# A Fourier filter and an expert layer on one core: the first batch on one filter tensor, its deferred loads, and new places in the plan

## The chip, the cores and the metric

The kernel runs on one core of a Trainium2 chip. The metric is the device time of one execution in microseconds (us), as the median of several runs. A profile records one execution: its span is shorter than the time by about 2 us. The engines of a core are PE (TensorE, matmuls), DVE (VectorE), ACT (ScalarE), POOL (GpSimd) and SP, which here only issues DMAs; PEld is TensorE's loading of weights, which overlaps PE. The granted clock is the share of TensorE's full clock that it was given.

## The reference, cut to what matters

```python
# x: 8 x 3008 x 256; filt_r, filt_i: 1505 x 256; w_in: 256 x 2048; w_out: 2048 x 256
X = np.fft.rfft(x, axis=1)
y = np.fft.irfft(X * (filt_r + 1j * filt_i), n=3008, axis=1)
h = y.reshape(24064, 256) @ w_in
g = h * (1.0 / (1.0 + np.exp(-beta * h)))
out = g @ w_out                                  # 24064 x 256, float32
```

## The kernel before

Both transforms are matmuls with sine tables, in two factors (3008 = 47 x 64). The expert layer is a main loop of 752 steps: 47 blocks of 512 tokens times 16 slices of the hidden width. A step is two matmuls into `hps`, a Silu on ACT giving `gT`, and, two steps later, four matmuls into `acc`. After 16 steps DVE copies `acc` to `ost` and it is stored. These stores serve below as milestones: store n is the start of DVE's first copy for block n.

The transforms of batches 1 to 7 are cut into units and placed between the steps by a plan: `s1` (first factor), a trip through DRAM (`d1`, read back as `a2`), `s23` (second factor, filter, inverse of it), a trip through `d2` (read as `zz`), `s4`. The views leave buffer numbers out: `a<-d` is the read of `a2` from `d1`, `zz<-d` that of `zz` from `d2`. Batch 0 has nothing to hide behind; it is computed first, with transposes in place of the DRAM trips.

```python
VLAG = 2                                  # s23: the inverse comes two units after the product
# start-up, in program order on POOL: loads of x, then these, then keep
for g in range(NG):
    load_filters(g, 0, nc.sync)           # both filter tensors, lower partitions
    load_filters(g, M, nc.gpsimd)         # both again, upper partitions (6.3 MB in all)
...                                       # w_in, four more issues on POOL
gp.tensor_scalar(keep[:], m_p[:], -1.0, float(M - 1), ALU.mult, ALU.add)
gp.tensor_tensor(keep[:], keep[:], m_p[:], ALU.mult)
gp.tensor_scalar(keep[:], keep[:], 0.5, None, ALU.is_gt)
...
def product(i):                           # batch 0: one product with each filter tensor
    ...
    nc.vector.tensor_tensor(p_t[:], pss[0][:], fr_sb[:, 2 * i : 2 * i + 2, :], ALU.mult)
    ...                                   # i == 0: q_t with keep
    nc.vector.tensor_tensor(q_t[:], pss[1][:], fi_sb[:, 2 * i : 2 * i + 2, :], ALU.mult)
...                                       # inverse3: p_t and q_t both times the one table t3
scale_wout(ws[0], 0, WG, nc.gpsimd); ...  # POOL; after the second of four, load_x(1)
...
place(1, 13, uz(1), per=1)                # rest of batch 0
place(14, 30, uz(2), per=1)
place(31, 50, uz(3), per=2)
place(16, 30, u1(1), per=2)               # batch 1
place(37, 37, [lambda: a2_read(1)], per=9)
place(41, 63, u23(1), True, per=2)
place(68, 68, [lambda: zz_read(1)], per=9)
place(71, 78, u4(1), per=2)
place(50, 70, u1(2), per=3)               # batch 2; x(b+1) is loaded at the end of u1(b)
```

## Time and profile before

| | before |
|---|---|
| time, median | 837.5 us (836.96 to 840.61, 3 runs) |
| span of the profiled run | 839.9 us |
| first `hps` matmul | 51.6 us |
| stores 7 to 43 (36 blocks) | 576.8 us |

Three lines of the page of the kernel before: the span; busy time and share of an engine; and the clock granted to PE in 40 slices of the span, in tenths of full speed.

```profile
span 839.9 us, 15300 instructions
PE 784.3 (93%) x5975; PEld 552.2 (66%) x6071; DVE 410.9 (49%) x670; ACT 585.7 (70%) x885; POOL 185.6 (22%) x200
...
PEclk9879999799999999999999999999999999999999
```

PE is the bound, but the clock dips early. Busy time by stretches of the kernel before shows where PE is idle (start:end in us, then the length; busy us of PE, PEld, DVE, ACT and POOL with counts; granted clock, DMA share, GB/s).

```profile
20.00:30.00 10.00, 2.96 (x27) 2.40 (x26) 1.63 (x5) 2.35 (x4) 5.46 (x11) 0.67 1.06 267
...
50.00:55.00 5.00, 4.61 (x28) 2.66 (x26) 1.98 (x4) 2.34 (x4) 5.00 (x9) 0.50 0.68 198
...
51.56:171.29 119.73, 99.15 (x714) 66.01 (x728) 69.47 (x110) 62.78 (x95) 51.47 (x49) 0.91 0.58 140
...
205.00:302.30 97.30, 95.18 (x726) 67.28 (x737) 51.90 (x81) 71.84 (x109) 19.39 (x20) 1.00 0.41 114
```

The third line runs from the first `hps` to the fifth store: PE is idle for 119.73 - 99.15 = 20.6 us there. The fourth is one steady batch: only 2.1 us idle.

In time order (start, duration, engine, line, operation; in brackets the idle time before it and what ended it), first POOL, then DVE of the kernel before:

```profile
27.05 0.71 POOL L203 DMA_DIRECT2D win_sb<-in_moe_w_in_dram  x1 [0.90 <-DMA fi_sb<-in_filt_i_dram]
27.85 0.18 POOL L230 TENSOR_SCALAR keep<-m_p 128x1 f32<-128x1 f32 x1
...
28.39 0.23 POOL L232 TENSOR_SCALAR keep<-keep 128x1 f32<-128x1 f32 x1
```

```profile
19.59 0.69 DVE L401 TENSOR_TENSOR pb_t<-ps,fr_sb 128x512 bf16<-128x512 f32 x1 [1.50 <-DMA fr_sb<-in_filt_r_dram]
...
28.66 0.48 DVE L403 SCALAR_TENSOR_TENSOR qb_t<-ps2q,keep,fi_sb 128x256 bf16<-128x256 f32 x1 [8.37 <-POOL keep L232]
...
45.67 0.68 DVE L408 TENSOR_TENSOR qb_t<-ps2q,fi_sb 128x512 bf16<-128x512 f32 x1
```

A 0.2 us operation holds DVE for 8.4 us, because POOL first issues twenty DMAs, and many of these wait for earlier ones to land. The chain of waits of the kernel before, followed back from the end, goes through the filters and not through `keep`:

```profile
15.55 17.22 DMA fi_sb<-in_filt_i_dram
...
32.79 10.36 DMA fi_sb<-in_filt_i_dram
```

Last, who PE waited for, as total, number and longest wait: from 52 to 205 us (two lines), then from 205 us to the end (the only line).

```profile
PE ps L489 <- DMA zz<-d: 10.1, 1, 10.1
...
PE ps L556 <- DMA a<-d: 2.4, 1, 2.4
```

```profile
PE ps L584 <- POOL v_t L574: 7.7, 6, 1.3
```

### The profile page before, as it was taken

The page shows a single profiled execution, that of the slowest core. Times are in us where ns is not written, and L with a number is a line of the kernel's source. Part 1 is how long each engine was busy: PE and PEld are TensorE (multiplying, and loading weights), DVE is VectorE, ACT ScalarE, POOL GpSimd, SP SyncE. Part 2 cuts the span into 40 slices and gives each one's busy share as a digit, 9 for nine tenths or more (in the row PEclk, how much of TensorE's full clock was granted, in tenths as well). Part 3 has the DMA queues.
Part 4 walks back from the last instruction along what each step waited for, and adds up shares of the span by engine and source line. Part 5 has one row for each costly group of instructions (what it writes and reads, how often), then busy time and mean ns, then how long its engine had stood idle before and what let it go on. Part 6 is the DMA issues. An engine that isn't in the chain of part 4 may idle for free.

```text
span 839.9 us, 15300 instructions
## 1 busy us (share of the span) xinstructions
PE 784.3 (93%) x5975; PEld 552.2 (66%) x6071; DVE 410.9 (49%) x670; ACT 585.7 (70%) x885; POOL 185.6 (22%) x200
## 2 busy tenths in 40 slices
PE   7589879599999999999999999999999999999997
PEld 4556645376667766777667866677667766766664
DVE  7536488367453656436562664536464463410101
ACT  6546556277767876678767777678766787677775
POOL 6279243023200431013210231003200232000000
PEclk9879999799999999999999999999999999999999
DMA  9962815912391118701293115911183022410101
GB/s 194 251 154 65 212 64 114 218 60 102 98 254 69 46 63 180 215 27 64 88 232 119 67 67 120 249 52 64 45 197 124 26 89 81 84 51 26 51 27 50
DMA packets 87426, 91.44 MB, mean 109 GB/s; under 512 B 4585, under 2 KB 76282, under 8 KB 87354
## 3 DMA queue, kind: packets, MB, share of 16 engines
q1 hardware_dynamic: 81274, 73.95, 29.7%
q0 software_dynamic: 6080, 16.52, 10.5%
q8 instruction: 47, 0.77, 0.4%
q14 instruction: 25, 0.20, 0.1%
HBM read 57.16 MB, written 46.66 MB: 124 GB/s over the span
## 4 chain that ended last, share of the span: by engine, by line
PE 82%; DMA 8%; DVE 5%; issue 3%; POOL 1%; ACT 0%; SPq 0%; DVEq 0%; POOLq 0%
PE acc L737 38%; PE hps L709 34%; DMA fi_sb<-in_filt_i_dram 3%; PE ps L489 3%; PE ps L532 3%; DVE ost L749 2%; PE ps L556 2%; PE ps L584 2%; DVE q_t L568 1%; POOL v_t L574 1%; DMA d<-a 1%; DVE p_t L566 1%; DMA d<-z 1%; DMA mark<-xg 1%; DMA xg<-in_x_dram 1%
## 5 line engine op out<-in xcount | busy, mean ns | idle before, releaser
L718 ACT ACTIVATE gT<-hps,beta_sb 128x512 bf16<-128x512 f32 x752 | 516.6, 687 | 211.7 <-PE hps L709 186.7
L737 PE MATMUL acc<-wout_sb,gT 128*128 128x256 bf16 x3008 | 457.8, 274 | 4.2 <-DVE ost L749 0.4
L709 PE MATMUL hps<-y,win_sb 128*128 128x512 bf16 (+7 forms) x1633 | 430.6, 352 | 0.7 <-issue 0.2
L737 PEld LDWEIGHTS <-gT 128*128 128x128 bf16 x3008 | 287.0, 98 | 140.6 <-issue 9.3
L574 POOL TENSOR_TENSOR v_t<-p_t,q_t 128x512 bf16<-128x512 f32 x84 | 106.5, 1267 | 401.6 <-DVE q_t L568 400.0
L709 PEld LDWEIGHTS <-win_sb 128*128 128x128 bf16 x1728 | 165.6, 98 | 25.3 <-issue 0.9
L749 DVE COPY ost<-acc 128x512 f32<-128x512 f32 x94 | 60.4, 683 | 200.4 <-PE acc L737 200.4
L568 DVE TENSOR_TENSOR q_t<-ps,fi_sb 64x512 f32<-64x512 f32 x168 | 115.7, 689 | 2.3
L107 DVE CAST a<-ps 96x512 bf16<-96x512 f32 x112 | 76.5, 686 | 68.9 <-PE ps L532 68.6
L109 DVE TENSOR_SCALAR y<-ps 128x376 bf16<-128x376 f32 x126 | 68.4, 548 | 79.2 <-PE ps L489 78.9
L566 DVE TENSOR_TENSOR p_t<-ps,fr_sb 128x512 f32<-128x512 f32 x84 | 58.1, 692 | 48.1 <-PE ps L556 46.7
L489 PEld LDWEIGHTS <-zz 96*128 96x128 bf16 x512 | 35.9, 101 | 39.2 <-DMA zz<-d 10.6
L105 ACT ACTIVATE z<-ps 128x512 bf16<-128x512 f32 x84 | 49.5, 590 | 11.8 <-PE ps L584 11.7
L489 PE MATMUL ps<-t,zz 96*128 96x94 bf16 x448 | 36.6, 208 | 10.9 <-DMA zz<-d 10.1
L532 PE MATMUL ps<-xg,t 94*96 94x512 bf16 x112 | 42.7, 383 | 2.9 <-ACT z L105 1.4
L584 PE MATMUL ps<-v_t,t 128*128 128x256 bf16 x168 | 32.1, 273 | 11.4 <-POOL v_t L574 8.4
L117 POOL DMA_DIRECT2D xg<-in_x_dram x32 | 17.6, 551 | 85.7 <-PE ps L532 72.1
L556 PE MATMUL ps<-a,t 128*128 128x256 bf16 x168 | 32.3, 274 | 3.5 <-DMA a<-d 2.4
L556 PEld LDWEIGHTS <-t 128*128 128x128 bf16 x168 | 15.9, 98 | 18.8 <-issue 5.4
L584 PEld LDWEIGHTS <-t 128*128 128x128 bf16 x168 | 15.2, 97 | 19.6 <-issue 9.3
L532 PEld LDWEIGHTS <-t 94*96 94x96 bf16 x112 | 13.8, 123 | 11.9
L143 POOL TENSOR_SCALAR wout_sb<-ws,rbeta_sb 128x256 bf16<-128x256 f32 x16 | 14.5, 921 | 17.2 <-DMA ws<-in_moe_w_out_dram 17.1
(107 smaller groups left out, 199.5 us busy)
## 6 DMA issues: line engine op xcount, KB each, us to landing
out_dram<-ost SPq DMA_DIRECT2D x41, 512.0 KB, 2.9
d<-a SPq DMA_DIRECT2D x28, 384.0 KB, 7.7
a<-d SPq DMA_DIRECT2D x28, 384.0 KB, 4.3
d<-z SPq DMA_DIRECT2D x28, 384.0 KB, 3.2
zz<-d SPq DMA_DIRECT2D x28, 384.0 KB, 8.9
xg<-in_x_dram POOLq DMA_DIRECT2D x32, 320.0 KB, 7.0
out_dram<-ost SPq DMA_DIRECT2D x20, 128.0 KB, 2.8
ws<-in_moe_w_out_dram SPq DMA_DIRECT2D x4, 512.0 KB, 7.1
```

What stands on the lines that cost most here:

```text
L107: nc.vector.tensor_copy(dst, src)
L109: nc.vector.tensor_scalar_mul(dst, src, scale)
L489: nc.tensor.matmul(ps[:, e, :NP], lhsT=zz[:, jj + e, dc * P : (dc + 1) * P], rhs=tab[:], start=True, stop=True,)
L532: nc.tensor.matmul(ps[:KP], lhsT=t1[:], rhs=s["x"][g][:, jj : jj + 2, :], start=True, stop=True)
L556: nc.tensor.matmul(ps[:, e, :], lhsT=t2[:, k0 + e, 1:3, :].rearrange("p c k -> p (c k)"), rhs=s["a2"][g][:, kk + e, :], start=True, stop=True,
L566: nc.vector.tensor_tensor(p_t[:], ps[:], fr_sb[:, k0 : k0 + 2, :], ALU.mult)
L568: nc.vector.tensor_tensor(q_t[to : to + M], ps[lo : lo + M], fi_sb[lo : lo + M, k0 : k0 + 2, :], ALU.mult,)
L574: nc.gpsimd.tensor_tensor(v_t[:], p_t[:], q_t[:], ALU.add)
L709: nc.tensor.matmul(hps[:, pos - t0 : pos - t0 + ln], lhsT=win_sb[:, dc, fb * P : (fb + 1) * P], rhs=ys[b][:, dc, n0 : n0 + ln], start=(dc ...
L718: nc.scalar.activation(gT[:, :tn], hps[:, :tn], ACT.Silu, scale=beta_sb[:, fb : fb + 1])
L737: nc.tensor.matmul(acc[tb // 2][:, tb % 2, :], lhsT=gT[:, tb * P : (tb + 1) * P], rhs=wout_sb[:, fb, :], start=(fb == 0 and tb % 2 == 0), ...
L749: nc.vector.tensor_copy(ost[:, 2 * h : 2 * h + n, :], acc[h][:, :n, :])
```

## The change

The intent: batch 0 needs one filter tensor only. Real filters sit on the lower and imaginary ones on the upper partitions of `fr_sb`; with a table that carries its parts in both orders and two inverse tables (`t3`, `t3b`), both products multiply by it. The other 3.1 MB of `fi_sb`, and the real filters for the upper half of `fr_sb`, are loaded in steps 1 to 7 from ACT's queue. `keep` is computed by DVE; x is one tile, loaded well ahead; batches 0 to 2 get new places; `VLAG` becomes 3. The diff, cut to its core:

```diff
-VLAG = 2
+VLAG = 3
-    vpool = pool("vpool", 3)
+    vpool = pool("vpool", 4)
-    t2 = consts.tile([P, NK, 3, M], BF16, name="t2", tag="t2")
+    t2 = consts.tile([P, NK, 5, M], BF16, name="t2", tag="t2")
     for g in range(NG):
-        load_filters(g, 0, nc.sync)
-        load_filters(g, M, nc.gpsimd)
+        load_filter(fr_sb, filt_r, 0, g * KG, KG, nc.sync)
+    for g in range(2):
+        load_filter(fr_sb, filt_i, M, g * KG, KG, gp)
+    angles(0, nc.vector)
+    ... keep on nc.vector ...
+    angles(1, gp)
+    for g in range(2, NG):
+        load_filter(fr_sb, filt_i, M, g * KG, KG, gp)
@@ product and inverse of batch 0 @@
+        for dst, ps in zip((p_t, q_t), pss):
+            nc.vector.tensor_tensor(dst[:], ps[:], fr_sb[:, 2 * i : 2 * i + 2, :], ALU.mult)
+        for src, tab in ((p_t, t3), (q_t, t3b)):
@@ after batch 0: x(1) first, then w_out; warm-up matmuls; the sign of t3's upper half @@
+        xs[1] = load_x(1, 2)
+    warm(4)
+    nc.vector.tensor_scalar_mul(t3[M:P], t3b[M:P], -1.0)
@@ s23 @@
+            nc.vector.scalar_tensor_tensor(
+                q_t[M:P], ps[:M], -1.0, fi_sb[:M, k0 : k0 + 2, :], ALU.mult, ALU.mult
+            )
@@ the plan (new places; those before are shown above) @@
+    place(1, 13, uz(1))
+    place(1, 7, uf(), per=2)          # fi_sb, and filt_r to fr_sb[M:], from nc.scalar
+    place(15, 29, uz(2))
+    place(34, 60, uz(3))
+        place(1, 15, u1(1), per=2)
+        place(20, 20, [lambda: a2_read(1)], per=9)
+        place(26, 56, u23(1), per=2)
+        place(60, 60, [lambda: zz_read(1)], per=9)
+        place(66, 78, u4(1), per=2)
+        place(36, 36, ux(2), per=9)
+        place(50, 66, u1(2, True), per=3)
+            place(a - 8, a - 8, ux(b + 1), per=9)     # x of later batches
```

More of the change, by code (lines that the diff above doesn't have):

```diff
@@ L72 @@
     wpool = pool("wpool", 1)
-    xpool = pool("xpool", 4)
+    xpool = pool("xpool", 1)
     apool = pool("apool", 4)
@@ L109, in evac, with load_x, load_filter @@
             nc.vector.tensor_scalar_mul(dst, src, scale)
-    def load_x(b):
-        xg = []
+    def load_x(b, n):
+        t = xpool.tile([NP, J, D], BF16, name="xg", tag="xg")
         xv = x[b].rearrange("(p j) d -> p j d", j=J)
-        for g in range(NJG):
-            t = xpool.tile([NP, JG, D], BF16, name="xg", tag="xg")
-            js = slice(g * JG, (g + 1) * JG)
-            nc.gpsimd.dma_start(t[:80], xv[:80, js, :])
-            nc.gpsimd.dma_start(t[80:NP], xv[80:NP, js, :])
-            xg.append(t)
-        return xg
-    def load_filters(g, at, eng):
-        k0 = g * KG
-        for f_sb, filt in ((fr_sb, filt_r), (fi_sb, filt_i)):
-            lo = AP(filt.tensor, filt.offset + k0 * D, [[N1 * D, H], [1, KG * D]])
-            hi = AP(
-                filt.tensor,
-                filt.offset + (N1 - k0) * D,
-                [[N1 * D, H], [-D, KG], [1, D]],
-            )
-            eng.dma_start(f_sb[at : at + H, k0 : k0 + KG, :].rearrange("p k d -> p (k d)"), lo)
-            eng.dma_start(f_sb[at + H : at + M, k0 : k0 + KG, :], hi)
+        for g in range(n):
+            js = slice(g * J // n, (g + 1) * J // n)
+            nc.gpsimd.dma_start(t[:80, js, :], xv[:80, js, :])
+            nc.gpsimd.dma_start(t[80:NP, js, :], xv[80:NP, js, :])
+        return t
+    def load_filter(f_sb, filt, at, k0, n, eng, later=False):
+        lo = AP(filt.tensor, filt.offset + k0 * D, [[N1 * D, H], [1, n * D]])
+        hi = AP(filt.tensor, filt.offset + (N1 - k0) * D, [[N1 * D, H], [-D, n], [1, D]])
+        units = [
+            lambda: eng.dma_start(
+                f_sb[at : at + H, k0 : k0 + n, :].rearrange("p k d -> p (k d)"), lo
+            ),
+            lambda: eng.dma_start(f_sb[at + H : at + M, k0 : k0 + n, :], hi),
+        ]
+        if later:
+            return units
+        for go in units:
+            go()
     def load_wout(f0, n):
@@ L168, in bits @@
         return tf
+    t3b = setup.tile([P, NK, P], BF16, name="t3b", tag="t3b")
     wz = setup.tile([P, 512], BF16, name="wz", tag="wz")
     nc.vector.memset(wz[:], 0.0)
-    pw = hpsum.tile([P, TB], F32, name="pw", tag="hps")
+    pw = [hpsum.tile([P, TB], F32, name="pw", tag="hps")]
     def warm(n, cols=512):
         for _ in range(n):
-            nc.tensor.matmul(pw[:, :cols], lhsT=wz[:, :P], rhs=wz[:, :cols], start=True, stop=True)
+            nc.tensor.matmul(pw[0][:, :cols], lhsT=wz[:, :P], rhs=wz[:, :cols], start=True, stop=True)
     ip = setup.tile([P, 1], I32, name="ip", tag="ip")
@@ L181 @@
     nc.gpsimd.iota(ic[:], pattern=[[1, P]], base=0, channel_multiplier=0)
-    x_cur = load_x(0)
+    x_cur = load_x(0, NJG)
     bt = setup.tile([NFB, P], F32, name="bt", tag="bt")
@@ L186 @@
     mark = dpool.tile([1, D], BF16, name="mark", tag="mark")
-    nc.sync.dma_start(mark[:], x_cur[2][:1, 0, :])
+    nc.sync.dma_start(mark[:], x_cur[:1, 2 * JG, :])
     gp = nc.gpsimd
@@ L194 @@
     for g in range(NG):
-        load_filters(g, 0, nc.sync)
-        load_filters(g, M, nc.gpsimd)
+        load_filter(fr_sb, filt_r, 0, g * KG, KG, nc.sync)
+    for g in range(2):
+        load_filter(fr_sb, filt_i, M, g * KG, KG, gp)
     WG = NFB // 4
     ws = [load_wout(i * WG, WG) for i in range(2)]
-    WI = 4
-    for h in range(WI):
-        fs = slice(h * FF // WI, (h + 1) * FF // WI)
-        nc.gpsimd.dma_start(
-            win_sb[:, :, fs], moe_w_in[:, fs].rearrange("(dc p) f -> p dc f", p=P)
-        )
     pre = small("pre")
@@ L227 @@
     )
-    m_p = bits("m_p", ip[:], ALU.bitwise_and, M - 1)
-    gp.tensor_scalar(keep[:], m_p[:], -1.0, float(M - 1), ALU.mult, ALU.add)
-    gp.tensor_tensor(keep[:], keep[:], m_p[:], ALU.mult)
-    gp.tensor_scalar(keep[:], keep[:], 0.5, None, ALU.is_gt)
     j_p = bits("j_p", ip[:], ALU.logical_shift_right, 2)
@@ L254, with angles @@
     us, rs = [], []
-    def angles(h):
+    def angles(h, eng):
         u = setup.tile([P, NH, M], F32, name="u", tag=f"u{h}")
         r = setup.tile([P, NH, M], F32, name="r", tag=f"r{h}")
-        nc.vector.tensor_tensor(
+        eng.tensor_tensor(
             u[:],
@@ L264, in angles @@
         )
-        nc.vector.tensor_scalar(r[:], u[:], ROUND_C, ROUND_C, ALU.add, ALU.subtract)
-        nc.vector.tensor_tensor(u[:], u[:], r[:], ALU.subtract)
+        eng.tensor_scalar(r[:], u[:], ROUND_C, ROUND_C, ALU.add, ALU.subtract)
+        eng.tensor_tensor(u[:], u[:], r[:], ALU.subtract)
         us.append(u)
@@ L273, in t2_part @@
         if part == 0:
-            nc.scalar.activation(t2[:, ks_, 1, :], u[:], ACT.Sin, scale=TWO_PI)
+            nc.scalar.activation(t2[:, ks_, 2, :], u[:], ACT.Sin, scale=TWO_PI)
         elif part == 1:
@@ L279, in t2_part @@
                 nc.scalar.activation(
-                    t2[:, ks_, 2, cols], r[:, :, cols], ACT.Sin, scale=sgn * TWO_PI, bias=b[:]
+                    t2[:, ks_, 1, cols], r[:, :, cols], ACT.Sin, scale=sgn * TWO_PI, bias=b[:]
                 )
@@ L284, in t2_neg @@
         ks_ = slice(h * NH, (h + 1) * NH)
-        nc.vector.tensor_scalar_mul(t2[:, ks_, 0, :], t2[:, ks_, 2, :], -1.0)
-    angles(0)
-    angles(1)
+        nc.vector.tensor_scalar_mul(t2[:, ks_, 4, :], t2[:, ks_, 1, :], -1.0)
+        nc.vector.tensor_copy(t2[:, ks_, 0, :], t2[:, ks_, 1, :])
+        nc.vector.tensor_copy(t2[:, ks_, 3, :], t2[:, ks_, 2, :])
+    angles(0, nc.vector)
+    m_p = bits("m_p", ip[:], ALU.bitwise_and, M - 1)
+    nc.vector.tensor_scalar(keep[:], m_p[:], -1.0, float(M - 1), ALU.mult, ALU.add)
+    nc.vector.tensor_tensor(keep[:], keep[:], m_p[:], ALU.mult)
+    nc.vector.tensor_scalar(keep[:], keep[:], 0.5, None, ALU.is_gt)
+    angles(1, gp)
+    for g in range(2, NG):
+        load_filter(fr_sb, filt_i, M, g * KG, KG, gp)
+    WI = 4
+    for h in range(WI):
+        fs = slice(h * FF // WI, (h + 1) * FF // WI)
+        gp.dma_start(win_sb[:, :, fs], moe_w_in[:, fs].rearrange("(dc p) f -> p dc f", p=P))
     a_t = ypool.tile([P, NDC, NK, J, 4], BF16, name="a_t", tag="y")
     def first1(i, on_act):
-        g, jj = divmod(4 * i, JG)
         for dc in range(NDC):
@@ L302, in first1 @@
                     ps[:, e, :KP],
-                    lhsT=x_cur[g][:, jj + e, dc * P : (dc + 1) * P],
+                    lhsT=x_cur[:, 4 * i + e, dc * P : (dc + 1) * P],
                     rhs=t1b[:],
@@ L312, in first1 @@
             )
-    for i in range(2):
+    for i in range(3):
         first1(i, (True, True))
@@ L317 @@
     t2_part(0, 0)
+    first1(3, (False, True))
+    warm(2)
     t2_part(0, 1)
-    for i in range(2, 4):
-        first1(i, (True, True))
-        warm(2)
-    t2_part(0, 2)
     first1(4, (False, False))
     warm(2)
-    for i in range(5, 8):
+    t2_part(0, 2)
+    first1(5, (False, False))
+    warm(2)
+    for i in range(6, 8):
         first1(i, (False, True))
@@ L328, with table3, turn_a @@
     t2_neg(0)
-    for part in range(3):
-        t2_part(1, part)
-    bps = hpsum.tile([P, NFB], F32, name="bps", tag="hps")
-    id_f = setup.tile([NFB, NFB], F32, name="id_f", tag="id_f")
-    nc.vector.tensor_copy(id_f[:], ident[:NFB, :NFB])
-    nc.tensor.transpose(bps[:], bt[:], id_f[:])
-    tiny = setup.tile([P, NFB], F32, name="tiny", tag="tiny")
-    nc.vector.tensor_copy(beta_sb[:], bps[:])
-    nc.vector.tensor_tensor(tiny[:], beta_sb[:], beta_sb[:], ALU.mult)
-    nc.vector.tensor_scalar(tiny[:], tiny[:], 1e-12, None, ALU.is_lt)
-    nc.vector.scalar_tensor_tensor(beta_sb[:], tiny[:], 2e-6, beta_sb[:], ALU.mult, ALU.add)
-    nc.vector.reciprocal(rbeta_sb[:], beta_sb[:])
-    nc.vector.tensor_copy(
-        t1.rearrange("p (a k) -> p a k", a=4), t1b.rearrange("p (k a) -> p a k", a=4)
-    )
-    t2_neg(1)
-    def table3(i):
-        pt = opsum.tile([P, 8, P], BF16, name="pt", tag="acc")
-        for e in range(8):
+    def table3(i, part, on_act):
+        pt = opsum.tile([P, KG, P], BF16, name="pt", tag="acc")
+        for e in range(KG):
             nc.tensor.transpose(
-                pt[:, e, :], t2[:, 8 * i + e, 1:3, :].rearrange("p c k -> p (c k)"), ident[:]
+                pt[:, e, :],
+                t2[:, KG * i + e, part : part + 2, :].rearrange("p c k -> p (c k)"),
+                ident[:],
             )
+        dst = t3 if part else t3b
         if i == 0:
-            evac(t3[:, 0, :], pt[:, 0, :], True, 0.5)
-            evac(t3[:, 1:8, :], pt[:, 1:8, :], True)
+            evac(dst[:, 0, :], pt[:, 0, :], on_act, 0.5)
+            evac(dst[:, 1:KG, :], pt[:, 1:KG, :], on_act)
         else:
-            evac(t3[:, 8 * i : 8 * i + 8, :], pt[:], True)
+            evac(dst[:, KG * i : KG * i + KG, :], pt[:], on_act)
     a2s = []
-    def turn_a(i):
+    def turn_a(i, on_act):
         if i % 2 == 0:
@@ L375, in turn_a, with beta_columns @@
                 )
-        evac(a2s[-1][:, 3 * (i % 2) : 3 * (i % 2) + 3, :], pb[:], i > 0)
+        evac(a2s[-1][:, 3 * (i % 2) : 3 * (i % 2) + 3, :], pb[:], on_act)
+    table3(0, 0, False)
+    turn_a(0, True)
+    turn_a(1, False)
+    table3(0, 2, True)
+    nc.vector.tensor_scalar_mul(fr_sb[M:P, 0, :], fr_sb[M:P, 0, :], keep[M:P])
+    def beta_columns():
+        bps = hpsum.tile([P, NFB], F32, name="bps", tag="hps")
+        id_f = setup.tile([NFB, NFB], F32, name="id_f", tag="id_f")
+        nc.vector.tensor_copy(id_f[:], ident[:NFB, :NFB])
+        nc.tensor.transpose(bps[:], bt[:], id_f[:])
+        tiny = setup.tile([P, NFB], F32, name="tiny", tag="tiny")
+        nc.vector.tensor_copy(beta_sb[:], bps[:])
+        nc.vector.tensor_tensor(tiny[:], beta_sb[:], beta_sb[:], ALU.mult)
+        nc.vector.tensor_scalar(tiny[:], tiny[:], 1e-12, None, ALU.is_lt)
+        nc.vector.scalar_tensor_tensor(
+            beta_sb[:], tiny[:], 2e-6, beta_sb[:], ALU.mult, ALU.add
+        )
+        nc.vector.reciprocal(rbeta_sb[:], beta_sb[:])
+        nc.vector.tensor_copy(
+            t1.rearrange("p (a k) -> p a k", a=4), t1b.rearrange("p (k a) -> p a k", a=4)
+        )
     z_t = ypool.tile([P, NDC, J, KP], BF16, name="z_t", tag="y")
@@ L386, in product @@
         pss = []
-        for part in (1, 0):
-            if part:
+        for part in (3, 1):
+            if part == 3:
                 ps = fpsum.tile([P, 2, D], F32, name="ps2", tag="f")
@@ L400, in product @@
             pss.append(ps)
-        nc.vector.tensor_tensor(p_t[:], pss[0][:], fr_sb[:, 2 * i : 2 * i + 2, :], ALU.mult)
-        if i == 0:
-            nc.vector.scalar_tensor_tensor(
-                q_t[:, 0, :], pss[1][:, 0, :], keep[:], fi_sb[:, 0, :], ALU.mult, ALU.mult
-            )
-            nc.vector.tensor_tensor(q_t[:, 1, :], pss[1][:, 1, :], fi_sb[:, 1, :], ALU.mult)
-        else:
-            nc.vector.tensor_tensor(q_t[:], pss[1][:], fi_sb[:, 2 * i : 2 * i + 2, :], ALU.mult)
+        for dst, ps in zip((p_t, q_t), pss):
+            nc.vector.tensor_tensor(dst[:], ps[:], fr_sb[:, 2 * i : 2 * i + 2, :], ALU.mult)
         pq[i] = (p_t, q_t)
@@ L414, in inverse3 @@
         ps = opsum.tile([P, 2, NDC, P], F32, name="psz", tag="acc")
-        for src in (p_t, q_t):
+        for src, tab in ((p_t, t3), (q_t, t3b)):
             for e in range(2):
@@ L420, in inverse3 @@
                         lhsT=src[:, e, dc * P : (dc + 1) * P],
-                        rhs=t3[:, k0 + e, :],
+                        rhs=tab[:, k0 + e, :],
                         start=src is p_t and dc == 0 and e == 0,
@@ L436, in table4 @@
             nc.scalar.activation(dst[:], tp[:], ACT.Copy)
-    for i in range(2):
-        turn_a(i)
-    table3(0)
     for i in range(NK // 2 + 1):
@@ L444 @@
         if i % 3 < 2 and i // 3 < 3:
-            turn_a(2 + 2 * (i // 3) + i % 3)
-        if i in (1, 2):
-            table3(i)
-        if i == 8:
+            turn_a(2 + 2 * (i // 3) + i % 3, True)
+        if i % 3 > 0 and i // 3 < 3:
+            table3(1 + i // 3, 4 - 2 * (i % 3), True)
+        if i in (1, 2, 3):
+            t2_part(1, i - 1)
+        if i == 2:
+            beta_columns()
+        if i == 3:
+            t2_neg(1)
+        if i == 9:
             table4()
@@ L451 @@
             inverse3(i - 1)
-    nc.gpsimd.tensor_scalar_mul(fi_sb[:, 0, :], fi_sb[:, 0, :], keep[:])
-    scale_wout(ws[0], 0, WG, nc.gpsimd)
-    ws.append(load_wout(2 * WG, WG))
-    scale_wout(ws[1], WG, WG, nc.gpsimd)
-    ws.append(load_wout(3 * WG, WG))
     xs = {}
     if B > 1:
-        xs[1] = load_x(1)
-    scale_wout(ws[2], 2 * WG, WG, nc.gpsimd)
-    scale_wout(ws[3], 3 * WG, WG, nc.gpsimd)
-    sp.close()
-    zpool = pool("zpool", 2)
-    zzpool = pool("zzpool", 4)
+        xs[1] = load_x(1, 2)
+    for i in range(4):
+        if i >= 2:
+            ws.append(load_wout(i * WG, WG))
+        scale_wout(ws[i], i * WG, WG, gp)
     ys = {}
@@ L473, with turn_z @@
     zz0 = {}
-    def turn_z(g, i):
-        if i == 0:
+    zz0[0] = apool.tile([KP, JG, D], BF16, name="zz", tag="a1")
+    def turn_z(g, i, on_act=False):
+        if g not in zz0:
             zz0[g] = zzpool.tile([KP, JG, D], BF16, name="zz", tag="zz")
@@ L483, in turn_z @@
                 )
-        evac(zz0[g][:, 4 * i : 4 * i + 4, :], pz[:KP], False)
+        evac(zz0[g][:, 4 * i : 4 * i + 4, :], pz[:KP], on_act)
     def last4(zz, tab, jj, dc, dst, on_act):
@@ L501, in last_z @@
         last4(zz0[g], t4b, 4 * jq, dc, yv[:, :, 4 * jq : 4 * jq + 4], on_act)
-    for i in range(2):
-        turn_z(0, i)
+    turn_z(0, 0)
+    turn_z(0, 1, True)
+    pw[0] = hpsum.tile([P, TB], F32, name="pw", tag="hps")
+    warm(4)
     for i in range(2 * NDC):
         last_z(0, i, i % 2 == 1)
-    for g in range(NG):
-        ks_ = slice(g * KG, (g + 1) * KG)
-        nc.gpsimd.tensor_scalar_mul(fi_sb[M:P, ks_, :], fi_sb[M:P, ks_, :], -1.0)
+        if i % 2:
+            warm(2)
+    nc.vector.tensor_scalar_mul(t3[M:P], t3b[M:P], -1.0)
+    sp.close()
+    zpool = pool("zpool", 2)
+    zzpool = pool("zzpool", 4)
     st = {}
@@ L532, in s1 @@
         nc.tensor.matmul(
-            ps[:KP], lhsT=t1[:], rhs=s["x"][g][:, jj : jj + 2, :], start=True, stop=True
+            ps[:KP], lhsT=t1[:], rhs=s["x"][:, 2 * i : 2 * i + 2, :], start=True, stop=True
         )
@@ L537, in s1 @@
             nc.sync.dma_start(s["d1r"][:, g * JG : (g + 1) * JG, :], s["a1"][:])
-            if g == NJG - 1 and b + 1 < B:
-                xs[b + 1] = load_x(b + 1)
     def a2_read(b):
@@ L557, in s23 @@
                     ps[:, e, :],
-                    lhsT=t2[:, k0 + e, 1:3, :].rearrange("p c k -> p (c k)"),
+                    lhsT=t2[:, k0 + e, 3:5, :].rearrange("p c k -> p (c k)"),
                     rhs=s["a2"][g][:, kk + e, :],
@@ L566, in s23 @@
             nc.vector.tensor_tensor(p_t[:], ps[:], fr_sb[:, k0 : k0 + 2, :], ALU.mult)
-            for lo, to in ((0, M), (M, 0)):
-                nc.vector.tensor_tensor(
-                    q_t[to : to + M],
-                    ps[lo : lo + M],
-                    fi_sb[lo : lo + M, k0 : k0 + 2, :],
-                    ALU.mult,
-                )
+            nc.vector.scalar_tensor_tensor(
+                q_t[M:P], ps[:M], -1.0, fi_sb[:M, k0 : k0 + 2, :], ALU.mult, ALU.mult
+            )
+            nc.vector.tensor_tensor(
+                q_t[:M], ps[M:P], fi_sb[M:P, k0 : k0 + 2, :], ALU.mult
+            )
             nc.gpsimd.tensor_tensor(v_t[:], p_t[:], q_t[:], ALU.add)
@@ L645, in uz, with uf, ux, go @@
         ]
-    place(1, 13, uz(1), per=1)
-    place(14, 30, uz(2), per=1)
-    place(31, 50, uz(3), per=2)
+    def uf():
+        units = []
+        for f_sb, filt, at in ((fi_sb, filt_i, 0), (fi_sb, filt_i, M), (fr_sb, filt_r, M)):
+            units += load_filter(f_sb, filt, at, 0, NK, nc.scalar, True)
+        units.append(lambda: gp.tensor_scalar_mul(fi_sb[:, 0, :], fi_sb[:, 0, :], keep[:]))
+        return units
+    def ux(b):
+        def go():
+            xs[b] = load_x(b, 1)
+        return [go]
+    place(1, 13, uz(1))
+    place(1, 7, uf(), per=2)
+    place(15, 29, uz(2))
+    place(34, 60, uz(3))
     first_step = [(S * b // TB) * NFB for b in range(B + 1)]
     if B > 1:
-        place(16, 30, u1(1), per=2)
-        place(37, 37, [lambda: a2_read(1)], per=9)
-        place(41, 63, u23(1), True, per=2)
-        place(68, 68, [lambda: zz_read(1)], per=9)
-        place(71, 78, u4(1), per=2)
+        place(1, 15, u1(1), per=2)
[3 more added lines that the diff above has]
+        place(66, 78, u4(1), per=2)
     if B > 2:
-        place(50, 70, u1(2), per=3)
-        place(77, 77, [lambda: a2_read(2)], per=9)
+        place(36, 36, ux(2), per=9)
+        place(50, 66, u1(2, True), per=3)
+        place(74, 74, [lambda: a2_read(2)], per=9)
     for b in range(2, B):
```

## The prediction

> **What bounds the kernel now.** The main loop is TensorE-bound: the page gives PE 784.3 of 839.9 us; a window over one steady batch (205 to 302 us) has 95.2 busy of 97.3. Three losses lie outside that.
>
> 1. Start-up. The first main-loop matmul (hps, L709) starts at 51.6 us in the timeline; the first batch's products end at 46.4. DVE waits 8.4 us (20.3 to 28.7) for the one-column keep: three POOL operations of 0.2 us, queued behind 16 filter and 4 w_in issues that wait for earlier DMAs. Then the filters are the limit: the chain of waits has fi_sb landing at 43.2 us, at 230 to 270 GB/s. The first steps run at a granted clock of 0.50 (50 to 55 us).
> 2. Batches 0 and 1 (52 to 205 us). Windows show about 20 us of idle PE: 10.1 before zz (147 to 157; d2 written in 7.6 us while x loads, then read in 4.2), about 7 in 105 to 135 where DVE is 75 to 96% busy with crowded s23 units, 2.4 for a2, and low clock after the gaps.
> 3. 1.3 us in each steady batch, PE L584 waiting for POOL v_t (near 207 us).
>
> **What the change does.**
> - The first batch needs only fr_sb: 3.1 MB of filters instead of 6.3, at 250 GB/s about 12.6 us less DMA. keep moves to DVE, early. Both stalls of point 1 go.
> - Added: 24 transposes, five more table evictions (about 0.7 us of ACT each, scaled from 1.02 for 1024 columns), four 0.36 us copies on DVE, half the angles on POOL (estimate 6 us, not critical); t2's second half and beta move into the product loop, which becomes bound by ACT (my sum: 17.5 us) and DVE (24 x 0.61 + 2.4 = 17 us), not DMA. Products start near 18 us, end near 36; hps starts near 41.3: 10 us gained. Warm-up matmuls keep the clock: 1.5 more. (The Trainium skill, "TensorE: Matmul & The Clock Gate", part 1: an idle array falls to half clock; the trace agrees with 0.50.)
> - 3.1 MB of filters return in steps 1 to 7 on ACT's queue: six issues of about 0.4 us, estimate 1 us lost; a2 at step 26 may still stall up to 3 us.
> - s23(1) is spread over steps 26 to 56 instead of 41 to 66, half of s1(2) is evicted by ACT, x(2) loads at step 36: the 7 us become about 3; zz's 10 about 3 (ten steps remain for write and read). About 12 gained with the clock.
> - VLAG 3: the v_t wait disappears, 1.3 x 6 = 7.8 us.
> - Negating scalar_tensor_tensor: about 0.07 us x 84 of DVE (483 against 414 ns at 256 columns), hidden. POOL's 16.3 us negation was hidden.
>
> **Sum.** 10 + 1.5 + 12 + 7.8 - 1 = 30 us, nearly all critical. 837.5 - 30 = 808; 2 us allowed for new stalls: **810 us, range 801 to 821**. Faster by over 2%: 0.89; within: 0.10; slower: 0.01.
>
> **What would show it.** First hps at 39 to 44 us; no DVE wait over 2 us among the products; steady batch 95.5 to 96.2 us, without v_t waits; PE idle from the first hps to the end of batch 1 some 8 us instead of 20; granted clock 1.0 in the first steps.
>
> **What would make it wrong.** ACT or a cold PE stretching the product loop past 20 us; ACT's filter issues blocking, so gT stalls PE in steps 1 to 7; filters, x(1), w_out and d1 sharing the DMA so that a2 or w_out come late; DVE still overfull in steps 26 to 50; zz still stalling PE.

## The result, and the profile after

| | before | after |
|---|---|---|
| time, median of 4 runs | 837.9 us | 803.4 us (800.89 to 806.49) |
| ratio | | 0.9585 (0.9544 to 0.9625) |
| first `hps` | 51.56 us | 43.39 us |
| first `hps` to store 5 | 119.73 us | 99.01 us |
| of it PE idle | 20.6 us | 6.6 us |
| stores 7 to 43 | 576.76 us | 566.79 us |

A ratio is the mean time of one kernel's fast runs over that of the other's in the same rounds, so it is not quite the ratio of the medians. A ratio of 0.9585 is a gain of 34.8 us on 837.9 us. Gains and losses of the experiments below are differences of ratios in the same way. They were run at other times. The two profiles differ by 38.4 us, since the profiled run of before was the slowest (841.7 us); read the profile for the places of the gain, and for its sizes within some 3 us.

From the page of the changed kernel:

```profile
span 801.5 us, 15281 instructions
PE 774.1 (97%) x6007; PEld 547.9 (68%) x6103; DVE 408.8 (51%) x670; ACT 589.0 (73%) x896; POOL 149.9 (19%) x148
...
PEclk9999999999999999999999999999999999999999
```

Its busy time by stretches (columns as above):

```profile
20.00:30.00 10.00, 6.96 (x102) 6.39 (x101) 8.27 (x22) 9.65 (x16) 3.94 (x7) 1.00 1.10 222
...
50.00:55.00 5.00, 4.56 (x32) 2.90 (x32) 3.36 (x6) 2.61 (x4) 3.32 (x4) 1.00 1.30 256
...
43.39:142.40 99.01, 92.45 (x715) 63.77 (x728) 65.23 (x103) 64.78 (x103) 25.55 (x25) 0.98 0.78 188
...
175.00:271.00 96.00, 95.19 (x730) 67.55 (x740) 52.17 (x82) 71.96 (x110) 16.30 (x14) 1.00 0.42 116
```

Between the first `hps` and store 5, 14.0 us of idle time went, and about the same matmuls took 99.15 - 92.45 = 6.7 us less at a mean clock of 0.98 instead of 0.91. Stores 13 and 19 are 95.66 us apart, where they were 97.28.

DVE of the changed kernel in time order: the start of the products, and their last one.

```profile
15.05 1.69 DVE L278 TENSOR_SCALAR t<-t 128x768 bf16<-128x768 bf16 x1
...
19.35 0.69 DVE L418 TENSOR_TENSOR pb_t<-ps,fr_sb 128x512 bf16<-128x512 f32 x1
...
38.03 0.68 DVE L418 TENSOR_TENSOR qb_t<-ps2q,fr_sb 128x512 bf16<-128x512 f32 x1
```

From the start of the first to the end of the last, the products now take 19.4 us instead of 26.8. What PE of the changed kernel waits for from 43 to 175 us (after 175 us the view has no line at all):

```profile
PE ps L567 <- DMA a<-d: 3.1, 2, 2.9
PE acc L763 <- DVE ost L775: 2.0, 2, 1.7
PE hps L735 <- ACT gT L744: 0.4, 1, 0.4
```

The waits for `zz` and `v_t` are gone. The one that remains has this chain behind it in the changed kernel:

```profile
49.17 14.26 DMA fr_sb<-in_filt_r_dram
...
63.43 9.22 DMA d<-a
...
72.74 3.37 DMA a<-d
```

The last deferred filter lands 14.3 us after its issue, and `a2` comes late. So the two readings to test are: which part earned what, and whether the DMA queues, rather than an engine, hold the first 75 us.

### The profile page after: what moved, and what is told of

Read it like the earlier page. It is cut to its first block, busy times and chain, and to the rows that moved or that the text cites. A ratio compares the mean times of both kernels' runs of the same rounds, so it can differ in the third digit from the quotient of the medians.

```text
span 801.5 us, 15281 instructions
## 1 busy us (share of the span) xinstructions
PE 774.1 (97%) x6007; PEld 547.9 (68%) x6103; DVE 408.8 (51%) x670; ACT 589.0 (73%) x896; POOL 149.9 (19%) x148
## 3 DMA queue, kind: packets, MB, share of 16 engines
q10 hardware_dynamic: 2496, 4.72, 2.7%
## 4 chain that ended last, share of the span: by engine, by line
PE 85%; DMA 6%; DVE 3%; issue 2%; ACT 2%; POOL 1%; DVEq 0%; ACTq 0%; POOLq 0%; SPq 0%
PE acc L763 39%; PE hps L735 35%; PE ps L545 3%; DMA d<-a 3%; PE ps L493 3%; PE ps L567 2%; PE ps L594 2%; DMA fr_sb<-in_filt_r_dram 2%; DVE ost L775 1%; DMA a<-d 1%; DMA xg<-in_x_dram 1%; ACT z_t L105 1%; ACT a L105 0%; DVE p_t L577 0%; DVE q_t L581 0%
## 5 line engine op out<-in xcount | busy, mean ns | idle before, releaser
L107 DVE CAST a<-ps 96x512 bf16<-96x512 f32 x104 | 71.0, 686 | 80.0 <-PE ps L545 79.9
L581 DVE TENSOR_TENSOR q_t<-ps,fi_sb 64x512 f32<-64x512 f32 x84 | 58.2, 693 | 1.2
L578 DVE SCALAR_TENSOR_TENSOR q_t<-ps,fi_sb 64x512 f32<-64x512 f32 x84 | 57.4, 684 | 1.1
L116 POOL DMA_DIRECT2D xg<-in_x_dram x12 | 6.9, 579 | 120.4 <-PE acc L763 97.8
```

Of the source, the lines that this page charges most:

```text
L107: nc.vector.tensor_copy(dst, src)
L581: nc.vector.tensor_tensor(q_t[:M], ps[M:P], fi_sb[M:P, k0 : k0 + 2, :], ALU.mult)
```

## The experiments

### One part undone, or one part alone

**VLAG back to 2.**

```diff
-VLAG = 3
+VLAG = 2
```

> The changed kernel with VLAG back at 2, all else as changed. Theory: the third step between s23's product and its inverse is what shortened each steady batch from 97.28 to 95.66 us, so the batch goes back to about 97.3, the 1.3 us waits for v_t return six times, and the time rises by 8 to 11 us, to about 813. Rival: the respaced loads of x (one tile, issued 56 steps ahead) or less POOL work shortened the batch; then the batch stays near 95.7 us and the time within 2 us of 803.

Measured: 812.3 us, ratio 0.9697 (0.9669 to 0.9726), 9.4 us more than changed. Stores 7 to 43 take 576.77 us again, and this is the only wait of PE after 175 us:

```profile
PE ps L594 <- POOL v_t L584: 7.7, 6, 1.3
```

The rival falls: the x loads and POOL's lighter work (and the fourth `v_t` buffer, which this run keeps) gave the steady batch nothing that can be seen.

**The kernel before with VLAG 3**, `vpool` with four buffers, nothing else.

> The kernel before with only VLAG 3 and one more v_t buffer. Theory: the same 8 to 10 us as in the changed kernel, about 828 to 830, steady batch 95.7 us. Rival: with the other parts as before the wait only moves to another instruction; then under 3 us.

Measured: 826.5 us, ratio 0.9859 (0.9833 to 0.9885), a gain of 11.8 us, a little above the 8 to 10 expected. Stores 7 to 47 take 621.9 us, as in the changed kernel, against 631.9 before. This part acts by itself.

**The kernel before with `keep` on DVE.**

```diff
-    gp.tensor_scalar(keep[:], m_p[:], -1.0, float(M - 1), ALU.mult, ALU.add)
-    gp.tensor_tensor(keep[:], keep[:], m_p[:], ALU.mult)
-    gp.tensor_scalar(keep[:], keep[:], 0.5, None, ALU.is_gt)
+    (the same three on nc.vector)
```

> The kernel before with only the three operations of keep moved from POOL to DVE. Theory: the 8.4 us wait of DVE goes, but the filters still land at about 43 us, so the products still end at 43 to 46 us and the time falls by 0 to 2 us. Rival: the wait for keep was the limit; then the first hps comes 6 to 8 us earlier and the time falls as much.

Measured: ratio 0.9997 (0.9966 to 1.0028), first `hps` at 51.96 us. DVE's longest wait in the start-up of before can be removed for nothing. DVE of this run shows what took its place:

```profile
21.22 0.69 DVE L401 TENSOR_TENSOR pb_t<-ps,fr_sb 128x512 bf16<-128x512 f32 x1 [2.49 <-DMA fr_sb<-in_filt_r_dram]
...
26.47 0.48 DVE L403 SCALAR_TENSOR_TENSOR qb_t<-ps2q,keep,fi_sb 128x256 bf16<-128x256 f32 x1 [4.56 <-DMA fi_sb<-in_filt_i_dram]
...
38.26 0.69 DVE L408 TENSOR_TENSOR qb_t<-ps2q,fi_sb 128x512 bf16<-128x512 f32 x1 [1.84 <-DMA fi_sb<-in_filt_i_dram]
...
43.66 0.69 DVE L408 TENSOR_TENSOR qb_t<-ps2q,fi_sb 128x512 bf16<-128x512 f32 x1 [1.73 <-DMA fi_sb<-in_filt_i_dram]
```

The last product still waits until 43.7 us for the filters.

**The changed kernel with `fi_sb` loaded early**, interleaved with `fr_sb` on SP and POOL as before; only the upper half of `fr_sb` stays in the loop.

> The changed kernel with the second filter tensor (fi_sb, 3.1 MB) loaded at the start again, interleaved with the first as before; only the third quarter (filt_r to the upper partitions, 1.6 MB) stays in the main loop. Theory: the volume ahead of the products is what held them, so they end near 45 us and the first hps comes 4 to 7 us later than 43.4; the wait for a2 (2.9 us) goes, so 2 to 5 us are lost in all. Rival: the deferral is worth nothing, the early keep and tables did it; then hps stays within 1.5 us of 43.4 and the time is the same or better by the 2.9 us.

Measured: 808.7 us, ratio 0.9645 (0.9624 to 0.9666), 5.0 us more than changed. The first `hps` comes at 47.1 us, 3.7 later (4 to 7 were expected), and the wait for `a2` is gone, as expected. DVE again waits for filters among the products, which end 3.8 us later:

```profile
DVE pb_t L421 <- DMA fr_sb<-in_filt_r_dram: 4.0, 2, 3.6
```

Not foreseen: the first store comes 11.8 us later (76.97 against 65.13), more than the 3.7. Part of that is this wait of PE, for w_out, which now stands behind the filters:

```profile
PE acc L766 <- POOL wout_sb L143: 4.4, 1, 4.4
```

By store 5 the loss is 8.3 us. Deferring the filters is worth about 5 us in time. Of the 8.2 us by which the first `hps` moved, this leaves some 4.4 to the other parts of the new start-up (tables, order of the loads, `keep`); no run takes these apart.

**The changed kernel with the old plan** of batches 0 to 2 and the old moments of the x loads.

> The changed kernel with the old plan of steps for batches 0 to 2 and the old moments of the x loads; tables, filters, VLAG 3 and warm-up as changed. Theory: the plan is what gained most of the 20 us between the first hps and the fifth store, so this loses 13 to 18 us (about 818), and the wait for zz near step 71 is back with 7 to 10 us. Rival: the gain there came from the tables, the moved filters and the warm clock; then under 5 us are lost.

Measured: 827.0 us, ratio 0.9863 (0.9837 to 0.9889): 23.3 us more than changed, above the expected 13 to 18; why it is more is not shown. From the first `hps` to store 5 it takes 122.8 us, of which PE is idle for 26.2, more than the 20.6 of before. The largest waits there:

```profile
PE ps L493 <- DMA zz<-d: 12.8, 1, 12.8
PE ps L567 <- DMA a<-d: 5.0, 1, 5.0
```

**The kernel before with the new plan alone.**

> The kernel before with only the new plan of steps for batches 0 to 2 and the new moments of the x loads; filters, tables, keep, VLAG 2 as before. Theory: taking the plan out of the changed kernel cost 23 us, and a plan acts by itself, so here it gains 16 to 23 us, to 815 to 821, with the wait for zz gone. Rival: the plan needs the earlier start or VLAG 3 to work (start-up and batch 1 share one chain); then under 12 us.

Measured: 829.8 us, ratio 0.9880 (0.9846 to 0.9915), a gain of 10.0 us only, where 16 to 23 were expected. The theory that the plan does all of this by itself is wrong; the rival had put the gain under 12. Its `s1(1)` now stands in step 2, but x(1) is still issued by POOL behind half of the w_out scaling, at 53 us. The largest waits of PE of this run between 45 and 205 us:

```profile
PE ps L532 <- DMA xg<-in_x_dram: 5.4, 1, 5.4
PE ps L489 <- DMA zz<-d: 2.7, 1, 2.7
PE ps L582 <- POOL v_t L572: 2.7, 2, 1.4
```

The first of them comes right at the start of the main loop, and the clock falls with it; busy time of this run in that stretch:

```profile
55.00:65.00 10.00, 5.87 (x32) 3.46 (x33) 3.54 (x6) 1.82 (x3) 9.88 (x14) 0.66 0.92 199
```

So the plan earns 10 us in the old kernel and 23 us in the new one. The new one gives it x(1) by step 2, by issuing that load before the scaling, and VLAG 3 covers the v_t waits of batch 1; its start-up is another one too. Which of these makes most of the difference was not separated.

**The kernel before with x(3) loaded at step 84** instead of after step 70.

> The kernel before with only the load of the fourth batch's x (x(3)) moved from step 70 to step 84, out of the way of the write of d2 and the read of zz. Theory: of the 10.1 us wait for zz, about 4 us come from this collision (d2 was written in 7.6 us against a median of 3.2) and about 6 from having only three steps between the read and its use; so the wait falls to 5 to 7 us and the time by 3 to 5 us. Rival A: the three steps alone make the wait; under 1 us gained. Rival B: the collision alone; 8 us or more gained.

Measured: 832.0 us, ratio 0.9937 (0.9917 to 0.9957), a gain of 5.3 us, just above the expected 3 to 5. The wait for `zz` is 4.0 us, where it was 10.1 and 5 to 7 were expected:

```profile
PE ps L489 <- DMA zz<-d: 4.0, 1, 4.0
```

The last write of `d2` to the issue of the `zz` read takes 2.6 us (141.5 to 144.2) instead of 7.7. So about six of the ten microseconds came from the x load running into that trip, the reverse of the expected split. The four that are left were put down to having only three steps for the read; that was not tested by itself. The changed kernel has neither wait.

### Parts of the start-up

**Without the eight warm-up matmuls** between the last products and the first `hps` (those ahead of the products stay).

> The changed kernel without the 8 warm-up matmuls between the last products and the first hps. Theory: the granted clock falls below 1.0 around 40 to 50 us and 1 to 3 us are lost. Rival: the first batch is now dense enough to keep the clock; then no loss, or 0.5 us gained.

Measured: 803.3 us, ratio 0.9588 (0.9562 to 0.9614), nothing lost; the clock stays 1.00 from 35 to 55 us. So it is not these matmuls that keep it; probably the product loop without its waits for filters does. In this stretch of that run PE was busy for 3.12 of 5 us, in pieces:

```profile
40.00:45.00 5.00, 3.12 (x39) 2.25 (x41) 2.48 (x5) 2.49 (x5) 0.23 (x1) 1.00 0.99 253
```

The kernel before looks much the same there, and yet its clock falls right after (a mean of 0.57 with two values, 1.00 and 0.50, puts the fall at 45.7 us):

```profile
40.00:45.00 5.00, 3.30 (x40) 2.69 (x39) 3.72 (x7) 2.10 (x6) 0.55 (x1) 1.00 0.87 228
45.00:50.00 5.00, 3.96 (x35) 3.01 (x34) 2.36 (x5) 1.25 (x3) 5.00 (x7) 0.57 0.08 19
```

The longest gap of PE between 30 and 45.7 us of the kernel before is 1.51 us. In the last 3.41 us ahead of the fall its PE was busy for 1.72 us; without warm-up the last two such stretches before 45.25 us have 2.26 and 2.31. So a fall needs no long gap, and a long gap need not bring one: in the run that follows, 3.6 us of waiting for `a2` (73.2 to 76.8 us) left the clock at 1.00, where in the changed kernel 2.9 us were followed by a mean of 0.83 from 75 to 85 us. What decides it is not shown.

**POOL's angles ahead of its second filter group.**

> The changed kernel with POOL's half of the angles moved ahead of its second filter group. Theory: the 1.69 us tensor_scalar on t2 (0.36 us elsewhere) waited for POOL's last subtraction, which then ends before 15 us; the products start 1 to 1.5 us earlier; but ACT bounds the loop after that, so the first hps moves by 0.5 to 1.5 us. Rival: the duration has nothing to do with POOL and stays at 1.7 us.

Measured: 803.9 us, ratio 0.9597 (0.9576 to 0.9619), no gain. But the duration in question is settled. DVE of this run:

```profile
15.31 0.35 DVE L278 TENSOR_SCALAR t<-t 128x768 bf16<-128x768 bf16 x1
...
18.27 0.69 DVE L418 TENSOR_TENSOR pb_t<-ps,fr_sb 128x512 bf16<-128x512 f32 x1
```

In the changed kernel the same instruction took 1.69 us, from 15.05 to 16.74, while POOL ran its subtraction from 14.73 to 16.53:

```profile
14.73 1.80 POOL L259 TENSOR_TENSOR u<-u,r 128x768 f32<-128x768 f32 x1
```

With POOL done at 14.4 it takes 0.35 us. This agrees with the Trainium skill, "SBUF — State Buffer", section "Who interferes with whom": VectorE in a two-port mode, which a `tensor_scalar` can enter, and GpSimd share a pair of ports under an exclusive lock, and whichever comes second stands still. The products start 1.1 us earlier, and yet the first `hps` comes at 43.95 us; in the loop DVE then waits 3.0 us for PE, where it waited 0.7. Of five profiles with the same start-up code the first `hps` comes between 42.2 and 45.0 us, so a gain of 1 us here would not be seen in one profile anyway.

### Is the early stretch held by DMA volume?

The Trainium skill, "DMA: Bandwidth & Descriptors", section "Issuing engines are not separate DMA queues", says that DMAs of SP, ACT and POOL run on the same 16 engines and interleave. Then the filters on ACT's queue delay `d1` on SP's, and the cure for the 2.9 us wait is less volume ahead of `a2`.

> The changed kernel once more, as the measure for the two variants of this call. About 803 us, ratio 0.957 to 0.961, first hps near 43.5 us, a wait for a2 of 3 to 4 us near 75 us.

Measured: 804.8 us, ratio 0.9587 (0.9568 to 0.9606); first `hps` at 45.0, the wait for `a2` 3.9 us:

```profile
PE ps L567 <- DMA a<-d: 4.1, 2, 3.9
```

The split of the filters is this edit:

```diff
-            units += load_filter(f_sb, filt, at, 0, NK, nc.scalar, True)
+            units += load_filter(f_sb, filt, at, 0, 2 * KG, nc.scalar, True)
+    def uf2(): ...                      # groups 2 and 3 of the three quarters, from nc.sync
+    place(27, 32, uf2(), per=9)
```

> The changed kernel with the deferred filters cut in two: frequencies 0 to 11 in steps 1 to 7 as now, 12 to 23 from the SP queue in steps 27 to 32, after a2 has been read. Theory: from 10 to 75 us the DMA queues are full, and what ends that stretch is a2; 2.4 MB fewer ahead of it bring a2 about 10 us earlier, the wait of 2.9 to 4 us goes, and the time falls by 2 to 4 us against the changed kernel. Rival: the wait is the latency of writing and reading d1, not the volume; then the wait stays over 2 us and so does the time.

Measured: 799.7 us, ratio 0.9546 (0.9523 to 0.9569), against the 0.9587 of the same rounds 3.4 us less; the two intervals touch. The longest wait for `a2` fell from 3.9 to 0.5 us:

```profile
PE ps L594 <- DVE q_t L581: 1.4, 2, 0.9
PE ps L567 <- DMA a<-d: 0.5, 1, 0.5
```

The `a2` read is issued 24.6 us after the first `hps` (66.85 - 42.21), where the changed kernel of the same call needs 29.6 (74.67 - 45.03). So it was volume, as the skill's page leads one to expect. The read comes 5 us earlier by this measure, where 10 were expected. Up to store 5, PE of this run is idle for 3.9 us instead of 6.5, and its matmuls take 2.7 us less at a clock of 1.00 instead of 0.97.

> The same with POOL's angles ahead of its second filter group and two of the three ACT passes over the second half of t2 moved ahead of the product loop, into ACT's 2.7 us idle gap. Theory: with the a2 wait gone, an earlier first hps is no longer given back; ACT has 1.5 us less in the loop and the products start 1 us earlier, so hps at 41 to 42.5 us and 1 to 2 us less than the split alone. Rival: the PSUM turns or the filter DMA hold the loop; then hps stays near 43.5 and the time equals the split alone.

Measured: 799.8 us, ratio 0.9532 (0.9513 to 0.9550). The rival holds: the first `hps` comes at 44.35 us, and the time equals the split alone. In the loop ACT no longer stalls DVE, but DVE waits 3.7 us for PE, and PE 2.4 us for DVE's copies of `t2`: the wait has only moved. Both variants beat the changed kernel by about 0.5% in the same rounds; the interval of the second (0.9513 to 0.9550) does not overlap that of the changed kernel (0.9568 to 0.9606).

## Why the prediction was right or wrong, point by point

It said 810 us, range 801 to 821. The time is 803.4 us, inside the range; the gain was 34.8 us by ratio, where the sum said 30 and the stated figure 27.5.

| term of the sum | predicted | measured, by profile |
|---|---|---|
| start-up to first `hps` | 10 us | 8.2 us (51.56 - 43.39) |
| clock in the first steps, batches 0 and 1 | 1.5 + 12 us | 20.7 us (119.73 - 99.01), 14.0 idle and 6.7 clock |
| VLAG, steady batches | 7.8 us | 10.0 us (576.76 - 566.79) |
| ACT's filter issues | -1 us | 0.4 us of PE waiting for gT (part of the 99.01) |

By these profiles the start-up brought less than was summed, the plan and VLAG more; the misses partly cancel.

- *The filters, not `keep`, are the limit after the stall.* Right: `keep` alone gained nothing, and early `fi_sb` in the changed kernel put the first `hps` back by 3.7 us. The other 4.4 us of the start-up are not taken apart.
- *Products near 18 to 36 us, first `hps` 41.3.* Measured 19.4 to 38.7 and 43.4, within the stated 39 to 44. The start was 1.3 us late: DVE's negation into `t2` stood still beside the angles on POOL. The prediction had this work down as "half the angles on POOL (estimate 6 us, not critical)" and missed the stall; for the time, "not critical" held, since removing the stall alone gains nothing.
- *No DVE wait over 2 us among the products.* Right; the longest was 1.2 us, for ACT's second half of `t2`.
- *Warm-up matmuls keep the clock.* Wrong as to cause. The clock was 1.00, but also without them. The rule quoted, that an idle array drops to half clock, fits the 0.66 after the wait of the plan alone (5.4 us idle). The 0.50 of before came without such a gap, after 3.4 us in which PE was busy for half the time; in the changed kernel PE was busier ahead of the first steps.
- *Batches 0 and 1, "about 12 gained with the clock".* The mechanism was right and the size was off: this is the mis-sized term, 20.7 us where 13.5 had been allowed. The wait for `zz` was put at 3 us left and none was left. The clock was the larger part of the miss: 6.7 us less matmul time for about the same matmuls (714 and 715 records), where 1.5 and a share of the 12 had been allowed. Some 3 us of the 20.7 may belong to the profiled run of before: the run with `keep` on DVE, with the same plan, takes 116.4 us from the first `hps` to store 5, not 119.7, and 97.5 of matmul time, not 99.2.
- *Spacing the plan does it.* Half right. The plan is worth 23 us in the changed kernel, but 10 us alone, where x(1) comes too late for step 2 (a wait of 5.4 us) and v_t waits remain. The prediction listed the parts as if they added up; its sum holds for the parts made together, and would have been wrong for the plan alone.
- *The wait for `a2` may still be 3 us.* Right: 2.9 us, by DMA volume, and a split of the filters takes it away. The volume itself was put too low: 3.1 MB were to return in the main loop, but the real filters for the upper half of `fr_sb` return too, and ACT's queue moved 4.72 MB.
- *VLAG removes 1.3 us in each steady batch.* Right in kind; the batch shortened by 1.62 us. With six of these the term is 9.7, and the wait view alone under-counts it by 0.3 us a batch.
- *The negating instruction costs 0.07 us more.* Wrong and harmless. It takes 684 ns against 693 for the plain product of that shape.

## What to carry to other kernels

A long wait in a profile may hide another one: here 8.4 us could be removed for nothing, because the bytes queued behind it arrived when they did before. Count the bytes that must land before a milestone, on all queues together, and move what is not needed until later; then look at what they collide with there. A plan of interleaved work should be tested with its inputs: placing units earlier helps only if their loads are earlier too, and a long gap that it leaves in PE can cost twice, as idle time and as clock.

## What the Trainium skill lacked or had wrong

- "TensorE: Matmul & The Clock Gate", part 1, agrees in kind: the clock averaged 0.66 over the 10 us that hold a PE gap of 5.4 us. Part 1 gives no amount up to which short gaps may add up: here the clock fell to half with no gap over 1.51 us in the 15 us before, after 3.41 us with 1.72 us busy, and stayed 1.00 with 2.26 and 2.31 us busy in such stretches.
- "SBUF — State Buffer", "Who interferes with whom", was right: 1.69 against 0.35 us for one bfloat16 `tensor_scalar` beside a POOL subtraction. The profile shows this as a long instruction, not as a wait; the section speaks of slower measurements, not of profiles.
- "DMA: Bandwidth & Descriptors", "Issuing engines are not separate DMA queues", was right: 2.4 MB of filters fewer ahead of `a2` cut the longest wait for it from 3.9 to 0.5 us, though they were on another engine's queue.
- "GPSIMD Engine Reference", section 3.1, measures `tensor_tensor` only, and as slower than VectorE. For a `tensor_scalar` with two operations it has no duration: 128x768 float32 took POOL 2.79 us, more than the subtraction of two tensors of that shape (1.80); VectorE took 0.73 for the same operation.
